# Threshold attention with a bilinear layer: two copies out of one product without an order between them, and loads of q and k that change places

## The chip, the cores and the metric

The kernel runs on one core of a Trainium2 chip. The metric is the device time of one execution in microseconds, as the median of several runs. A core has five engines that work side by side, each through its own instructions in order: PE (TensorE, matmuls; its loads of weights are listed as PEld), ACT (ScalarE), DVE (VectorE), POOL (GpSimd) and SP (SyncE, which issues nearly all transfers here). They wait for each other through semaphores.

## The reference

```python
def _attn_ref(q, k, v, tau):                 # 8 batches x 8 heads, 576 rows, 64 columns
    scale = 1.0 / np.sqrt(q.shape[-1])
    scores = scale * np.matmul(q, k.transpose(0, 1, 3, 2))
    thresh = np.max(scores, axis=-1, keepdims=True) - tau
    scores = np.where(scores >= thresh, scores, -1000000000.0)
    scores = scores - np.max(scores, axis=-1, keepdims=True)
    attn = np.exp(scores)
    attn = attn / (np.sum(attn, axis=-1, keepdims=True) + 1e-09)
    return np.matmul(attn, v)

def _moe_ref(x, w_a, w_b, w_out):            # x: 4608 x 512; w_a, w_b: 512 x 1536; w_out: 1536 x 512
    return (x @ w_a) * (x @ w_b) @ w_out
```

The attention's result, with the heads of a row side by side, is x. All numbers are fp32.

## The kernel before, in words

Two heads of a batch make a pair: 32 pairs, four to a batch. A pair's 576 rows of q are cut into units u = 0 to 3 of 128 rows and a last one of 64, the tail (u = 4). All matmuls are 64 x 64 tiles[...]. The main loop runs over slots g, one unit of attention each. In a set of four pairs there are 20 slots: first (pair, 0) and (pair, 1) for each of the four pairs in slots 0 to 7, then (pair, 2), (pair, 3), (pair, 4) for each in slots 8 to 19. The next set follows.

A slot's work in the order in which it is written:

- `scores` (L352): matmuls of qT and kT into two PSUM tiles sc (one for the tail); then on DVE the row maximum (L359) and the threshold (L360).
- `turn_blocks` for the unit of the slot before: DVE transposes its weights in 32 x 32 blocks (L446), SP writes them to DRAM (`swap`, L457). `turn_back` later reads them back as wT (L466, L469).
- a part of the bilinear layer (`advance`): matmuls into pab (L626, L699) and po (L756, L802), a share of them at four places of each slot, set by a pace.
- `weigh`: ACT's exp (L380), DVE's masking with the row sums (L383).
- `prep`: on DVE, the transposition (L320) in 32 x 32 blocks of rows of q or k that a later slot needs. Of a pair, q comes in two loads: q0 (rows for u = 0, 1; 128x256 in SBUF) and q1 (the rest; 128x320); k comes in one (128x576).
- `weighted`, where a part is due: the product of the turned weights with v into the PSUM tile pv (L483), 36 matmuls, and `settle`, which copies it into x. Parts are due three slots after units u = 1 and u = 4, that is in slots 4, 6, 8, 10 (a half of 256 rows) and 13, 16, 19 and 2 of the next set (the other half and the tail, 320 rows).
- the sums' reciprocals on DVE (L394, L396) and ACT's normalising (L402).
- `load` (L147): SP issues four transfers for q0, k or q1 of a later pair; `load_v` (L170); stores of results (L826).

Before the change, q0 of a pair is loaded four slots ahead of its first unit and turned two ahead; k is loaded three ahead and turned one ahead. The tiles of q rotate over two buffers, those of k over four.

All PSUM tiles (sc, pv, pab, po, tp) come from one pool of four tiles of two banks. A new tile waits for those who read the one whose place it takes. A part of the layer with seven products in place of eight holds up to two of the four over longer stretches.

`settle` takes pv in two halves: with its first half ACT fills the first columns of x's tile (L490), with the second half DVE fills the rest, in two copies of 64 rows, as the two heads stand crossed there (L492). Where a tail is due, `settle` is called twice on the same pv, for xT and for xt. The tile layer records an order between the copies of the two engines, since they touch the same tiles, so ACT goes first, then DVE, and with a tail ACT and DVE once more. When a batch's half of x is complete, POOL copies it with the two 64-row halves exchanged (xS, L500), for the layer.

At the end `keep_order` fixes the order on every engine as written.

Of the kernel before, what the change touches and what calls it, by code (L numbers as in the profile page):

```python
# [52 lines left out]
def kernel(  # L53
# [38 lines left out]
    nc = tc.nc  # L92
    B, H, S, D = q.shape
    P = 128
# [6 lines left out]
    TAIL = S - MAIN  # L101
# [7 lines left out]
    GT = HALF // TAIL  # L109
# [16 lines left out]
    def banks(n, name):  # L126

        return psum.tile([P, 2, 512], FP32, tag="banks", name=name)[:, :, 0:n]
# [152 lines left out]
    for _ in range(TW_BUFS):  # L281
        t = work.tile([P, 2 * NB, Q], FP32, tag="tw", bufs=TW_BUFS, name="rows")
# [31 lines left out]
    x_of, xtail_of = {}, {}  # L314
# [123 lines left out]
    def width(i, h):  # L438
        return (HALF, HALF, TAIL)[h] if i < HP else (HALF, HALF + TAIL)[h]
# [35 lines left out]
    def product(wT, vm, n):  # L475

        pv = banks(n // 2, "pv")
        for s in range(NSLOT):
            for j in range(2):
                rows = slice(j * D, (j + 1) * D)  # L480
                for c in range(2):
                    y = j ^ c
                    nc.tensor.matmul(pv[c * D:(c + 1) * D, y], vm[rows, s], wT[y](rows, s),  # L483
                                     start=(s == 0), stop=(s == NSLOT - 1))
        return pv

    def settle(out, pv, c0, c1):

        n = c1 - c0
        nc.scalar.copy(out[:, 0:n], pv[:, 0, c0:c1])  # L490
        for c in range(2):
            nc.vector.tensor_copy(out[c * D:(c + 1) * D, n:2 * n], pv[(1 - c) * D:(2 - c) * D, 1, c0:c1])  # L492

    def x_tile(name):
        return work.tile([P, HP, HALF], FP32, tag="xT", bufs=XT_BUFS, name=name)

    def exchange(x, xs, hp, c0, c1, engine):

        for r in range(2):
            engine.tensor_copy(xs[r * D:(r + 1) * D, hp, c0:c1], x[(1 - r) * D:(2 - r) * D, hp, c0:c1])  # L500
# [17 lines left out]
    def weighted_unit(i, u):  # L518

        b, hp = pairs[i]  # L520
        wT = turned.pop((i, u, "pe"))
        pv = product([lambda rows, s, t=t: t[rows, s] for t in wT], loaded[i]["v"], P)
        if (b, 0) not in x_of:
            x_of[b, 0] = x_tile("xT")
            state["xs"] = x_tile("xS")
        settle(x_of[b, 0][:, hp, u * P:(u + 1) * P], pv, 0, D)
        exchange(x_of[b, 0], state["xs"], hp, u * P, (u + 1) * P, nc.gpsimd)
        if hp == HP - 1:
            state["rows"] = u + 1
            if u == 0:  # L530
                blocks.append(((x_of[b, 0], state["xs"]), ("first", b, 0)))

    def weighted(i, h):

        b, hp = pairs[i]
        n = width(i, h)
        if h < 2:
            groups = G + (n > HALF)
            wT = [turned.pop((i, 2 * h + y))[:, 0:groups] for y in range(2)]
        else:  # L540
            t = turned.pop((i, NT))
            wT = [t[:, y:y + 1] for y in range(2)]
        pv = product([lambda rows, s, t=t: t[rows, :, s] for t in wT], loaded[i]["v"], n)
        if h < 2:
            if hp == 0:
                x_of[b, h] = x_tile("xT")
            settle(x_of[b, h][:, hp, :], pv, 0, P)
            if hp == HP - 1:
                complete.append((x_of.pop((b, h)), ("half", b, h)))
        if n % HALF:  # L550
            t = b % GT
            if hp == 0 and t == 0:
                xtail_of[b // GT] = x_tile("xt")
            settle(xtail_of[b // GT][:, hp, t * TAIL:(t + 1) * TAIL], pv, (n - TAIL) // 2, n // 2)
            del loaded[i], prepared[i]
            if hp == HP - 1 and t == GT - 1:
                complete.append((xtail_of.pop(b // GT), ("tail", b - t, 0)))
# [325 lines left out]
    def backlog():  # L883
        return (len(blocks) + len(complete)) * cost() + (running["left"] if running["ffn"] is not None else 0)
# [28 lines left out]
    n = 0  # L913
# [4 lines left out]
    for g in range(len(units) + PV_LAG):  # L918
        written = len(pending)
        state["converted"] = state["added"]  # L920
        here = g < len(units)
        converting = bool(early.get(g)) or bool(early.get(g - 1))
        if here:
            i, u = units[g]
            scores(i, u)
        exchange_blocks()
        pace = (PACE if g > BY_PE else PACE_EARLY) * BLOCK_COLS
        if g > BY_PE:
            pace = min(pace, backlog() / (min([a for a in arrivals if a > g] + [len(units) + PV_LAG + 1]) - g))
        pace += NSLOT * S / 2 / (NT + 1) + CATCH_UP * max(backlog() - BLOCK_COLS, 0)  # L930
        if 2 <= g < BY_PE + 2:
            weighted_unit(*units[g - 2])
            running["owed"] -= NSLOT * P // 2
        if g < 3:
            prep_copy(*prep_pe(g + 1, "q"))
        convert_rest(g, 0)
        if g == 0:
            for c in range(0, 2 * QUARTER - 2 * CW + 1, 2 * CW):
                extra.append(more_u32[:, c:c + 2 * CW].rearrange("p (f w) -> p f w", w=2))
        if g == 3:  # L940
            for c in range(0, NSUM - 2 * CW + 1, 2 * CW):
                extra.append(sums_u32[:, c:c + 2 * CW].rearrange("p (f w) -> p f w", w=2))
        load_weights(RAWS)
        if g > BY_PE and g <= len(units):
            turn_blocks(*units[g - 1])
        if g > BY_PE:
            advance(PORTIONS[0] * pace)
        if here:
            weigh(i, u)
        if here and g < BY_PE:  # L950
            reciprocal(i, u, nc.vector)
        if 0 < g <= BY_PE:
            turn_pe(*units[g - 1])
        if g < 3:
            prep_copy(*prep_pe(g + 1, "k"))
        for p in range(HP, NPR):
            for name, d in (("q0", 2), ("k", 1), ("q1", 1)):
                if g == (second if name == "q1" else first)[p] - d:
                    prep(p, name)
        if g > BY_PE:  # L960
            advance(PORTIONS[1] * pace)
            n = g - PV_LAG
            if BY_PE <= n < len(units) and part(*units[n]):
                p, h = part(*units[n])
                if pairs[p][1] == 0:
                    make_x(2 if h == 1 and p >= HP and pairs[p][0] % GT == 0 else 1)
                make_room()
                weighted(*part(*units[n]))
                running["owed"] -= NSLOT * width(*part(*units[n])) // 2
            if BY_PE + 1 < g <= len(units) + 1:  # L970
                turn_back(*units[g - 2])
        for n in early.get(g, [])[:1]:
            convert_first(n)
            convert_clamp(n)
        if here and g < BY_PE:
            diagonals(i, u)
        elif here:
            reciprocal(i, u, nc.scalar if converting else nc.vector)
            normalise(i, u)
        convert_rest(g, 1)  # L980
        if g <= BY_PE:
            advance(pace)
        convert_rest(g, 2)
        for n in early.get(g, [])[1:]:
            convert_first(n)
            convert_clamp(n)
        load_weights(RAWS)
        for p in range(HP, NPR):
            for name, d in (("q0", 4), ("k", 3), ("q1", 3)):
                if g == (second if name == "q1" else first)[p] - d:  # L990
                    load(p, name)
        for p in range(1, NPR):
            if g == first[p] - 1:
                load_v(p)
        if BY_PE <= g < BY_PE + HP:
            load_v(g - BY_PE, again=True)
        store(written)
        if g > BY_PE:
            advance(PORTIONS[2] * pace)
            advance(PORTIONS[3] * pace)  # L1000

        if not converting and not state["sums"]:
            state["slots"] = state.get("slots", 0) + 1
            for n in {1: (0,), 2: (1,), 3: (2,)}.get(state["slots"], ()):
                for z in range(2):
                    weight_sums(n, z)
            if state["slots"] >= 3 and state["through"]:
                for z in range(2):
                    weight_sums(3, z)
                state["sums"] = True  # L1010
        if g > first[HP] + 1 and not converting and state["first"] < 3 * SEVENS:
            first_sums(state["first"] % 3, state["first"] // 3)
            state["first"] += 1
# [37 lines left out]
```

## Time and profile before

| | |
|---|---|
| median of three runs | 1477.29 us (1473.63 to 1477.57) |
| the profiled execution | 1482.24 us, its span 1480.5 us |
| busy: PE, PEld | 1394.5 us (94%), 1257.0 us (85%) |
| busy: DVE, ACT, POOL | 1010.0 us (68%), 684.8 us (46%), 480.1 us (32%) |
| granted TensorE clock, mean | 0.988 |
| DMA | 223.21 MB, mean 151 GB/s |
| start (0 to 185 us): PE busy | 148.78 us |
| middle (185 to 1345 us): PE busy | 1116.03 us |
| end (1345 to 1480 us, the layer alone): PE busy | 129.66 us |

The span runs from the first to the last instruction; the execution's own time has the start and the end around it. A row of the costliest groups reads: line, engine, operation, tile written <- tiles read, shapes, count | busy time, mean length in ns | idle time of the engine ahead of these instructions, and what ended most of it. A row of waits reads: engine, line, what ended the wait, then the total, the count and the longest in us. A wait for several semaphores is put down to one of them. The lengths of matmuls are modelled, and they overlap.

### The profile page before, as it was taken

The page shows a single profiled execution, that of the slowest core. Times are in us where ns is not written, and L with a number is a line of the kernel's source. Part 1 is how long each engine was busy: PE and PEld are TensorE (multiplying, and loading weights), DVE is VectorE, ACT ScalarE, POOL GpSimd, SP SyncE. Part 2 cuts the span into 40 slices and gives each one's busy share as a digit, 9 for nine tenths or more (in the row PEclk, how much of TensorE's full clock was granted, in tenths as well). Part 3 has the DMA queues.
Part 4 walks back from the last instruction along what each step waited for, and adds up shares of the span by engine and source line. Part 5 has one row for each costly group of instructions (what it writes and reads, how often), then busy time and mean ns, then how long its engine had stood idle before and what let it go on. Part 6 is the DMA issues. An engine that isn't in the chain of part 4 may idle for free.

```text
span 1480.5 us, 76328 instructions
## 1 busy us (share of the span) xinstructions
PE 1394.5 (94%) x34208; PEld 1257.0 (85%) x34208; DVE 1010.0 (68%) x2245; ACT 684.8 (46%) x1243; POOL 480.1 (32%) x668
## 2 busy tenths in 40 slices
PE   5789999998999999999999899999999989999998
PEld 4678687887889988899998787988888968999998
DVE  5798687777867786586756577667766677654223
ACT  4787455545545454454444444445545445441110
POOL 2674623423060506033324224150505060605000
PEclk9899999999999999999999999999999999999999
DMA  9877677668756775577556676467755676551000
GB/s 211 201 206 189 164 172 191 170 163 194 176 147 157 169 199 149 138 171 180 144 131 139 151 171 165 117 171 163 188 140 141 166 176 169 136 137 41 4 18 17
DMA packets 325080, 223.21 MB, mean 151 GB/s; under 512 B 169616, under 2 KB 308880, under 8 KB 324752
## 3 DMA queue, kind: packets, MB, share of 16 engines
q1 hardware_dynamic: 322384, 217.73, 60.0%
q8 instruction: 269, 4.41, 1.3%
q10 hardware_dynamic: 2368, 0.59, 0.2%
q14 instruction: 59, 0.48, 0.1%
HBM read 128.58 MB, written 89.65 MB: 147 GB/s over the span
## 4 chain that ended last, share of the span: by engine, by line
PE 79%; DVE 6%; DMA 5%; issue 3%; SPq 3%; ACT 2%; POOL 1%; ACTq 0%; DVEq 0%; POOLq 0%
PE pab L626 25%; PE pab L699 18%; PE po L756 17%; PE pv L483 9%; PE sc L352 9%; DMA wT<-swap 2%; DVE mx L359 2%; SPq L457 1%; DMA kT<-in_k_dram 1%; DVE tw L446 1%; POOL kept L725 1%; PE po L802 1%; DVE xT L492 1%; PE tp L427 1%; DVE tw L383 0%
## 5 line engine op out<-in xcount | busy, mean ns | idle before, releaser
L402 ACT ACTIVATE tw<-tw,rcp 128x576 f32<-128x576 f32 x272 | 197.8, 769 | 219.0 <-DVE rcp L396 219.0
L359 DVE TENSOR_REDUCE mx<-sc 128x1 f32<-128x576 f32 x288 | 205.3, 749 | 125.2 <-PE sc L352 121.6
L380 ACT ACTIVATE tw<-sc,bias,scalars 128x576 f32<-128x576 f32 x288 | 239.4, 831 | 9.8 <-ACT bias L379 0.2
L592 POOL TENSOR_TENSOR h<-h,u 128x512 f32<-128x512 f32 x28 | 35.1, 1276 | 628.7 <-DVE h L669 491.0
L383 DVE SCALAR_TENSOR_TENSOR tw<-sc,thr,tw 128x576 f32<-128x576 f32 x288 | 223.6, 799 | 14.7 <-ACT tw L380 14.5
L756 PE MATMUL po<-wo_sb,h 64*64 64x256 f32 x3264 | 222.2, 377 | 0.0
L352 PE MATMUL sc<-kT,qT 64*64 64x288 f32 x2016 | 190.9, 405 | 17.2 <-ACT xt L490 6.8
L446 DVE STREAM_TRANSPOSE tw<-tw 128x576 f32<-128x576 f32 x272 | 196.1, 754 | 0.8 <-ACT tw L402 0.8
L483 PE MATMUL pv<-wT,vm 64*64 64x160 f32 (+3 forms) x5184 | 180.8, 274 | 12.1 <-DMA wT<-swap 7.7
L756 PEld LDWEIGHTS po<-wo_sb,h 64*64 64x64 f32 x3264 | 171.0, 133 | 20.9
L483 PEld LDWEIGHTS pv<-wT,vm 64*64 64x64 f32 x5184 | 164.6, 134 | 22.3 <-issue 9.9
L756 PE MATMUL po<-sums_u,h 64*64 64x256 f32 x2448 | 164.8, 379 | 2.5 <-DVE h L707 2.5
L725 POOL TENSOR_TENSOR h<-h 128x256 f32<-128x256 f32 x168 | 117.4, 731 | 115.8 <-PE po L756 101.9
L352 PEld LDWEIGHTS sc<-kT,qT 64*64 64x64 f32 x2016 | 112.2, 133 | 42.0 <-ACT xt L490 16.5
L756 PEld LDWEIGHTS po<-sums_u,h 64*64 64x64 f32 x2448 | 126.1, 134 | 19.5 <-DVE h L707 3.2
L492 DVE COPY xT<-pv 64x128 f32<-64x128 f32 (+1 forms) x136 | 38.1, 280 | 141.5 <-ACT xT L490 140.4
L626 PE MATMUL pab<-xU,wb_sb 64*64 64x128 f32 x4096 | 133.3, 270 | 0.3 <-issue 0.2
L626 PEld LDWEIGHTS pab<-xU,wb_sb 64*64 64x64 f32 x4096 | 126.6, 133 | 3.7 <-issue 0.7
L379 ACT ACTIVATE bias<-mx,scalars 128x1 f32<-128x1 f32 x288 | 82.9, 288 | 91.2 <-DVE mx L359 90.9
L626 PE MATMUL pab<-xS,wa_sb 64*64 64x128 f32 x2048 | 110.7, 270 | 3.1 <-POOL xS L500 1.5
L490 ACT COPY xT<-pv 128x128 f32<-128x128 f32 (+1 forms) x68 | 17.6, 260 | 202.8 <-PE pv L483 202.7
L699 PE MATMUL pab<-xS,wb_sb 64*64 64x256 f32 (+1 forms) x1536 | 100.1, 363 | 0.0
(137 smaller groups left out, 2427.2 us busy)
## 6 DMA issues: line engine op xcount, KB each, us to landing
swap<-tw SPq DMA_DIRECT2D x480, 144.0 KB, 2.6
wT<-swap SPq DMA_DIRECT2D x120, 576.0 KB, 4.6
vm<-in_v_dram SPq DMA_DIRECT2D x128, 72.0 KB, 3.3
swap<-tw SPq DMA_DIRECT2D x128, 72.0 KB, 1.8
kT<-in_k_dram SPq DMA_DIRECT2D x112, 72.0 KB, 4.4
wT<-swap SPq DMA_DIRECT2D x56, 144.0 KB, 2.9
out_dram<-kept SPq DMA_DIRECT2D x30, 256.0 KB, 4.1
qT<-in_q_dram SPq DMA_DIRECT2D x112, 40.0 KB, 4.3
```

Source lines behind the costliest of these rows:

```text
L352: nc.tensor.matmul(sc[j if u < NT else 0][to, c], qT[r, q0:q0 + D], kT[r, c * SH:(c + 1) * SH], start=True, stop=True)
L359: nc.vector.tensor_reduce(mx[:, c], sc[j], axis=AX.XY, op=ALU.max)
L379: nc.scalar.activation(bias[:, j:j + 1], mx[:, j:j + 1], AF.Copy, scale=e_nscale)
L380: nc.scalar.activation(wb[j], sb[j], AF.Exp, bias=bias[:, j:j + 1], scale=e_scale)
L383: nc.vector.scalar_tensor_tensor(out=wv, in0=sb[j], scalar=thr[:, j:j + 1], in1=wv, op0=ALU.is_ge, op1=ALU.mult, accum_out=sums[:, j:j + 1])
L402: nc.scalar.activation(w, w, AF.Copy, scale=rcp[:, j:j + 1])
L446: nc.vector.transpose(w, w)
L483: nc.tensor.matmul(pv[c * D:(c + 1) * D, y], vm[rows, s], wT[y](rows, s), start=(s == 0), stop=(s == NSLOT - 1))
L626: nc.tensor.matmul(out[c * D:(c + 1) * D, r, f * P:(f + 1) * P], w[g][k][rows, w0:w0 + D], moving[k][rows], start=(fresh and k == 0 and f ...
L699: nc.tensor.matmul(pab[c * D:(c + 1) * D, r], w[rows, f // n, k, fs + c * D:fs + (c + 1) * D], moving, start=(k == 0), stop=(k == H - 1))
L725: (nc.vector if state["over"] else nc.gpsimd).tensor_tensor(*a, **kw)
L756: nc.tensor.matmul(po[c * D:(c + 1) * D, r, y], ht[rows, t0:t0 + D], other[rows, f], start=(f == 0), stop=(f == NF // 2 - 1))
```

## The change

The copies of `settle` are declared independent of each other where they are on different engines: ACT's copies and DVE's copies of one pv no longer wait for one another, also across the two calls for a half and a tail (they share the lists in `read`). Waits of the copies for the product, and of readers for the copies, stay. Then the slots: q0 is loaded three slots ahead of a pair's first unit and turned one ahead, k is loaded four ahead and turned two ahead. q1 stays.

```diff
-    def settle(out, pv, c0, c1):
+    def settle(out, pv, c0, c1, others):
 
         n = c1 - c0
-        nc.scalar.copy(out[:, 0:n], pv[:, 0, c0:c1])
-        for c in range(2):
-            nc.vector.tensor_copy(out[c * D:(c + 1) * D, n:2 * n], pv[(1 - c) * D:(2 - c) * D, 1, c0:c1])
+        one = [nc.scalar.copy(out[:, 0:n], pv[:, 0, c0:c1])]
+        two = [nc.vector.tensor_copy(out[c * D:(c + 1) * D, n:2 * n], pv[(1 - c) * D:(2 - c) * D, 1, c0:c1])
+               for c in range(2)]
+        for mine, theirs in ((one, others[1] + two), (two, others[0] + one)):
+            for a in mine:
+                for b in theirs:
+                    tc.declare_no_dep(a.ins, b.ins, reason="banks of their own")
+        others[0].extend(one)
+        others[1].extend(two)
...
-        settle(x_of[b, 0][:, hp, u * P:(u + 1) * P], pv, 0, D)
+        settle(x_of[b, 0][:, hp, u * P:(u + 1) * P], pv, 0, D, ([], []))
...
+        read = [], []
...
-            settle(x_of[b, h][:, hp, :], pv, 0, P)
+            settle(x_of[b, h][:, hp, :], pv, 0, P, read)
...
-            settle(xtail_of[b // GT][:, hp, t * TAIL:(t + 1) * TAIL], pv, (n - TAIL) // 2, n // 2)
+            settle(xtail_of[b // GT][:, hp, t * TAIL:(t + 1) * TAIL], pv, (n - TAIL) // 2, n // 2, read)
...
-            for name, d in (("q0", 2), ("k", 1), ("q1", 1)):
+            for name, d in (("q0", 1), ("k", 2), ("q1", 1)):
                 if g == (second if name == "q1" else first)[p] - d:
                     prep(p, name)
...
-            for name, d in (("q0", 4), ("k", 3), ("q1", 3)):
+            for name, d in (("q0", 3), ("k", 4), ("q1", 3)):
                 if g == (second if name == "q1" else first)[p] - d:
                     load(p, name)
```

## The prediction

> **What bounds the kernel now.** I read the page's busy shares first, then the windows of three stretches, the list of waits, and last the timeline at each wait of PE.
>
> ```profile
> PE 1394.5 (94%) x34208; PEld 1257.0 (85%) x34208; DVE 1010.0 (68%) x2245; ACT 684.8 (46%) x1243; POOL 480.1 (32%) x668
> ...
> L492 DVE COPY xT<-pv 64x128 f32<-64x128 f32 (+1 forms) x136 | 38.1, 280 | 141.5 <-ACT xT L490 140.4
> ...
> L490 ACT COPY xT<-pv 128x128 f32<-128x128 f32 (+1 forms) x68 | 17.6, 260 | 202.8 <-PE pv L483 202.7
> ```
>
> ```profile
> 185.00:1345.00 1160.00, 1116.03 (x27777) 1003.47 (x27773) 821.49 (x1840) 552.15 (x985) 363.70 (x531) 1.00 0.65 160
> ```
>
> PE is the bound, at a granted clock of 1.00 in the long middle stretch, where attention and layers run side by side. All that this change can win there are PE's pauses: 1160.0 - 1116.0 = 44 us. ACT waits for the product with v, and DVE then waits for ACT (140.4 us of idle). Most of that idle is the product itself; what matters is the end of the pair of copies, and who waits for it:
>
> ```profile
> PEld sc L352 <- ACT xt L490: 16.5, 8, 2.1
> ...
> PE sc L352 <- ACT xt L490: 6.8, 4, 1.7
> ...
> PE sc L352 <- DVE xt L492: 4.6, 3, 1.7
> ```
>
> The scores wait for the copies: their second PSUM tile takes the one that pv has just used. One such place in the timeline (start, length, engine, operation, idle before it):
>
> ```profile
> 307.20 0.27 ACT L490 COPY xT<-pv 128x128 f32<-128x128 f32 x1 [4.96 <-PE pv L483]
> 307.50 0.59 DVE L492 COPY xT<-pv 64x128 f32<-64x128 f32 x2 [2.55 <-ACT xT L490]
> ...
> 308.12 0.18 ACT L490 COPY xt<-pv 128x32 f32<-128x32 f32 x1 [0.66 <-DVE xT L492]
> 308.34 0.39 DVE L492 COPY xt<-pv 64x32 f32<-64x32 f32 x2 [0.25 <-ACT xt L490]
> ...
> 308.94 0.95 PE L352 MATMUL sc<-kT,qT 64*64 64x288 f32 x11 [1.61 <-ACT xt L490]
> ```
>
> The two engines work in strict turn, ACT, DVE, ACT, DVE, from 307.20 to 308.73, and PE goes on 0.2 us later. The wait is put down to ACT, but it is DVE's copy that ended last. The second pause that the change touches:
>
> ```profile
> 340.62 0.77 DVE L320 STREAM_TRANSPOSE kT<-kT 128x576 f32<-128x576 f32 x1
> ...
> 341.46 0.60 PEld L352 LDWEIGHTS sc<-kT,qT 64*64 64x64 f32 x12 [0.95 <-issue]
> ```
>
> The scores of a pair start when its keys are turned (340.62 + 0.77 = 341.39); the profile says "issue", but the end of the turn lies 0.07 us ahead.
>
> **What the Trainium skill says.** "PSUM — Partial Sum Buffer", section "Specifications (TRN2)": ScalarE and VectorE read PSUM in parallel at full bandwidth as long as they don't meet in one bank. ACT reads the first bank of pv, DVE the second. The trace before agrees for other tiles: ACT's exp out of sc at 339.01 (0.83 us, mean of its row 0.831) overlaps DVE's masking out of the other sc at 338.91 (0.80, mean 0.799). "Perfetto Trace Analysis", section "Optimization Strategy": the same gap coming back on the busiest engine can mean too few buffers for the next tile. The trace agrees: eight waits of some 2 us on ACT's xt copy, all at a tile that takes pv's PSUM. The same page, section "DMA Instruction — HWDGE (DVE, Sync)": a transfer's semaphore wait is spent on the issuing sequencer, ahead of the start that is shown, so what is queued behind it stands too. SP's wait at L147, shown below, agrees.
>
> **The change, part by part.**
>
> *A. The order between the copies goes.* No instruction is added or removed: 68 + 32 copies on ACT, 136 + 64 on DVE. DVE now waits for the product itself. In the place above DVE would run from 307.20: 0.59 + 0.02 + 0.39 = 1.00, to 308.20, while ACT needs 0.27 + 0.18 = 0.45. The last end falls from 308.73 to 308.20: **0.53 us** where a tail goes with the half (0.30 from the start, 0.23 from the turn in the middle); without a tail **0.30 us** (ACT's 0.27 and 0.03 of handing over). This needs a DVE that is idle when the product ends: its idle of 140.4 us in 61 waits is 2.3 us each, so it is, outside the first 100 us, where DVE is busy and 8 products gain next to nothing. I followed every pause of PE over 0.3 us in the timeline. It ends 0.10 to 0.22 us after the last copy in 14 places:
> - nine with a tail, at 308.94, 441.52, 599.77, 823.34, 853.13, 996.74, 1021.75, 1161.43 and 1302.57, each with 1.2 to 2.1 us between two matmul starts, so more than 0.53: 9 x 0.53 = 4.8 us;
> - five without, at 370.35, 528.15, 709.27, 922.00 and 1085.12 (0.34 to 1.34 us): 5 x 0.30 = 1.5 us.
>
> Indirect, where the copies are a link further back: POOL's exchange L500 waits for DVE's copy in 7 places (14.6 us) and PE then for xS, at most 7 x 0.30 = 2.1; from 210 to 262 us the chain that ended last passes through three settles (220.19, 234.93, 249.87) and on through DVE to the swap transfers, 3 x 0.30 = 0.9; four pauses that end on DVE's masking after such a slot (292.56, 314.17, 334.17, 630.24), 4 x 0.30 = 1.2. Together 0 to 4.2; I take half, 2.1, since POOL's copies and DVE's other work bound some of them.
>
> *B. Rows of q and keys change places.* On DVE a turn of q0 takes 0.44 (128x256) and one of k 0.77, 28 of each. Counting slots in a set of four pairs (20 slots), q0 was turned in slots 18, 0, 2, 4 and k in 19, 1, 3, 5; now the reverse. The turn that stands just ahead of a pair's first scores becomes 0.33 us shorter. That pause shows four times (341.49, 501.02, 661.03, 836.36, with 0.55 to 0.90 us): 4 x 0.33 = 1.3 us. The longer turn goes to the even slots. Queued behind it on DVE are the copies out of pv (slots 2 and 4), the sums and reciprocals and, through them, ACT's normalising. In slots 2 and 4 DVE stood idle for 0.8 us or more ahead of the product's end every time (least at 1037.6 and 1203.1), so 0.33 is covered; without that cover it would be 12 x 0.33 = 4 us at worst.
>
> On SP four issues of k (0.63 us each) and four of q0 (0.46) change places. Before, three of four q0 loads stood at SP for their buffer, which the next slot's scores still read:
>
> ```profile
> SPq L147 <- PE sc L352: 8.8, 9, 2.5
> ```
>
> A slot later that buffer is free, so these waits go. Queued behind them are the stores of results, and then the next slot's swaps, which wait for DVE anyway (L457 on L446, 331.9 us in 107 waits): I take 0, with bounds of 1 us gained and 1 us lost (the k issues take 4 x 0.17 = 0.7 us longer in three slots of 20 and as much less in the next, where v is loaded too). k has four buffers, freed at least three slots ahead. Landing: k, in the place that q0 takes, landed 3.5 us or more ahead of its turn each time (the closest landed at 322.29, turned at 325.81), and q0 is the smaller load; no wait on a landing comes in.
>
> *Sum.* 4.8 + 1.5 + 1.3 = 7.6 direct, 2.1 indirect. Of a pause removed, a part comes back: PE reaches the next wait sooner, and some of these (PE on wT<-swap, 13.3 us with the weights' side in 12 waits) hang on SP and transfers. I take back 2.2, three tenths of the direct sum. That leaves **-7.5 us**. The profiled execution has a span of 1480.5, 1482.24 with what lies around it, 5 us above the median of the three runs, 1477.29. The difference is put to the median: **1469.8**.
>
> **Rivals.**
> 1. *The gain comes back elsewhere (or the order isn't lifted, since both engines write one xT tile).* If the pauses move to the next wait, a third is left, -2.5; if only B acts, -1.3. Time 1474.8 to 1476.0. For it: DMA's mean busy share is 0.65 in the stretch, and PE still waits for transfers. Against it: those transfers start from DVE's turns, which follow the scores on PE, so the chain moves as a whole.
> 2. *Slower: two readers of pv hold each other up.* One mechanism: ACT and DVE read the two halves of pv and write one xT at the same time, which no trace of before shows for this tile. If DVE's two copies take twice as long (1.18 and 0.78), a settle with a tail ends after 1.98 instead of 1.53 us, one without after 1.18 instead of 0.89: 9 x 0.45 + 5 x 0.29 = 5.5, half as much again indirectly, less the 1.3 of B: +7 us, 1484. It decides from copies that are longer by half (0.30 of 0.59). Against it: the banks differ, and exp and masking overlap unhurt. Short of that point it takes from the gain only.
> 3. *More than forecast.* If all indirect links count and nothing comes back: -11.8, and 1 us from SP: 1464.5.
>
> **How the numbers follow.** A change under 0.3% (4.4 us) can't be told from none in this kernel, whose runs before differ by 3.9 us. The forecast case has 0.55, the third 0.12, the first 0.23, the second 0.10. Their own ends spread over the bound: faster 0.64, same 0.26, slower 0.10. For 8 in 10 the range takes in the third case with its spread of runs and most of the first: 1461 to 1478.
>
> **What would show it.** Right: DVE's row L491 (the copies' new line) waits for PE pv and no longer for ACT; the idle 18.4 us of ACT's xt for DVE's xT is gone; PE's pauses after a product with a tail fall from about 2.0 to 1.5 us; SP's wait at the loads for PE sc is near nothing; the four pauses behind the keys' turn are under 0.6 us. Wrong: copies longer than 0.28 us on DVE, or PE's idle of 44 us in the middle stretch unchanged, with larger rows for wT<-swap or DVE's masking.

## The result and the profile after

The changed kernel took **1464.73 us** (median of 6 runs, 1457.75 to 1467.37), the kernel before on the same chip 1476.54 us (6 runs, 1473.16 to 1477.57). The ratio is **0.992** [0.9896, 0.9945], 11.8 us less. Two further comparisons of the same two kernels, told below, gave 0.9939 [0.9918, 0.996] and 0.9942 [0.9919, 0.9966], 8.4 and 8.6 us less. The forecast was 1469.8, 7.5 us less.

The profiled execution of the changed kernel took 1467.37 us, its span 1465.6. First the busy shares, then two of the costliest groups (the copies of `settle` are now at L490 and L491):

```profile
PE 1387.9 (95%) x34208; PEld 1248.2 (85%) x34208; DVE 1014.9 (69%) x2245; ACT 682.9 (47%) x1243; POOL 479.5 (33%) x668
...
L491 DVE COPY xT<-pv 64x128 f32<-64x128 f32 (+1 forms) x136 | 38.1, 280 | 120.3 <-PE pv L483 119.1
...
L490 ACT COPY xT<-pv 128x128 f32<-128x128 f32 (+1 forms) x68 | 17.6, 258 | 206.0 <-PE pv L483 205.9
```

The counts are the same. DVE's copies have the same length (280 ns before and after), but what ends the idle time before them is now the product (119.1 us of it), not ACT: the order is gone, and the two readers of pv don't slow each other. This fits the Trainium skill, "PSUM — Partial Sum Buffer", section "Specifications (TRN2)", which has ScalarE and VectorE read PSUM in parallel at full bandwidth without a bank collision, now also for this tile.

The middle stretch by windows (length, then busy time of PE, PEld, DVE, ACT, POOL):

```profile
185.00:1335.00 1150.00, 1114.66 (x27736) 1012.14 (x27732) 823.99 (x1840) 549.50 (x984) 362.26 (x535) 1.00 0.65 161
```

PE is idle here for 1150.0 - 1114.7 = 35.3 us, where it was 44.0: 8.7 us less, at the same mean clock of 1.00. (The window ends 10 us sooner, as the stretch does.) In the two later profiles of the changed kernel it was 38.2 and 39.8 us, that is 5.8 and 4.2 less: the size differs from one execution to the next. From the ninth slot (slot 8) to the end, the span is 9.9 us shorter; the other 5.0 of the 14.9 us between the two spans lie ahead of slot 8, which began at 82.5 before and at 77.5 after. The granted clock (the third number from the end) was another in the first part of the run, as the windows from 40 to 80 us show, of before and of after:

```profile
40.00:80.00 40.00, 28.57 (x678) 25.14 (x678) 30.78 (x73) 28.50 (x60) 25.29 (x31) 0.87 0.85 194
```

```profile
40.00:80.00 40.00, 31.43 (x846) 27.07 (x848) 34.34 (x82) 32.64 (x70) 27.93 (x33) 0.96 0.93 226
```

0.96 in place of 0.87 over 40 us is 3.6 us at most, an estimate that takes PE to set the pace throughout; from 80 to 185 us it was 1.00 in place of 0.97. An experiment below asks whether the change has a part in it.

The waits of PE and PEld on the copies, and SP's at the loads:

```profile
PEld sc L352 <- ACT xt L490: 12.3, 8, 1.6
...
PE sc L352 <- ACT xt L490: 4.7, 4, 1.2
...
PE sc L352 <- DVE xt L491: 3.2, 3, 1.1
```

```profile
SPq L170 <- DMA wT<-swap: 13.2, 18, 1.2
...
SPq L147 <- PE sc L352: 2.3, 4, 1.2
```

The three rows have the same counts as before, and each wait is about half a microsecond shorter (longest 2.1 to 1.6, 1.7 to 1.2, 1.7 to 1.1). SP's wait at the loads for the scores fell from 8.8 us in 9 to 2.3 in 4, as forecast, but a wait later in the queue grew (L170, loads of v, 3.5 us in 4 before, 13.2 in 18 now), so that SP's waits at the two together did not fall.

The place of the timeline that the prediction showed, five microseconds sooner:

```profile
302.23 0.27 ACT L490 COPY xT<-pv 128x128 f32<-128x128 f32 x1 [4.97 <-PE pv L483]
302.23 0.59 DVE L491 COPY xT<-pv 64x128 f32<-64x128 f32 x2 [2.27 <-PE pv L483]
302.39 0.19 ACT L490 COPY xt<-pv 128x32 f32<-128x32 f32 x1
302.84 0.39 DVE L491 COPY xt<-pv 64x32 f32<-64x32 f32 x2
...
303.50 0.95 PE L352 MATMUL sc<-kT,qT 64*64 64x288 f32 x11 [1.13 <-ACT xt L490]
```

Both engines start at 302.23. DVE ends at 302.84 + 0.39 = 303.23, 1.00 us after the start in place of 1.53, and PE's idle is 1.13 in place of 1.61. The wait is still put down to ACT, which ended at 302.58; the copy that PE waits for is DVE's.

And the turn ahead of a pair's first scores, which is now one of q0:

```profile
334.49 0.44 DVE L320 STREAM_TRANSPOSE qT<-qT 128x256 f32<-128x256 f32 x1
...
335.00 0.67 PEld L352 LDWEIGHTS sc<-kT,qT 64*64 64x64 f32 x13 [0.61 <-issue]
```

The turn takes 0.44 in place of 0.77, and the idle time of PEld behind it is 0.61 in place of 0.95.

Of PE's pauses, taken as the time between two matmul starts, the same places add up so:

| pauses | before | after | less | forecast |
|---|---|---|---|---|
| 9 after a product with a tail | 17.5 us | 12.9 us | 4.6 us | 4.8 us |
| 5 after one without | 3.74 us | 2.50 us | 1.24 us | 1.5 us |
| 4 behind the turn of a pair | 2.75 us | 1.37 us | 1.4 us | 1.3 us |

### The profile page after: what moved, and what is told of

Its sections match the earlier page's. It is cut to its first block, busy times and chain, and to the rows that moved or that the text cites. A ratio compares the mean times of both kernels' runs of the same rounds, so it can differ in the third digit from the quotient of the medians.

```text
span 1465.6 us, 76332 instructions
## 1 busy us (share of the span) xinstructions
PE 1387.9 (95%) x34208; PEld 1248.2 (85%) x34208; DVE 1014.9 (69%) x2245; ACT 682.9 (47%) x1243; POOL 479.5 (33%) x668
## 4 chain that ended last, share of the span: by engine, by line
PE 78%; DVE 7%; DMA 5%; SPq 5%; issue 3%; ACT 1%; POOL 1%; ACTq 0%; DVEq 0%; POOLq 0%
PE pab L633 24%; PE pab L706 18%; PE po L763 17%; PE pv L483 9%; PE sc L352 9%; DMA wT<-swap 2%; SPq L457 2%; DVE mx L359 2%; SPq L147 1%; DMA qT<-in_q_dram 1%; DVE tw L446 1%; DVE tw L383 1%; PE po L809 1%; SPq L225 1%; POOL kept L732 0%
## 5 line engine op out<-in xcount | busy, mean ns | idle before, releaser
L352 PE MATMUL sc<-kT,qT 64*64 64x288 f32 x2016 | 192.0, 405 | 10.5 <-ACT xt L490 4.7
L446 DVE STREAM_TRANSPOSE tw<-tw 128x576 f32<-128x576 f32 x272 | 196.0, 754 | 0.8 <-ACT tw L402 0.8
L763 PEld LDWEIGHTS po<-wo_sb,h 64*64 64x64 f32 x3264 | 167.4, 133 | 24.9
L491 DVE COPY xT<-pv 64x128 f32<-64x128 f32 (+1 forms) x136 | 38.1, 280 | 120.3 <-PE pv L483 119.1
L490 ACT COPY xT<-pv 128x128 f32<-128x128 f32 (+1 forms) x68 | 17.6, 258 | 206.0 <-PE pv L483 205.9
```

What stands on the lines that cost most here:

```text
L352: nc.tensor.matmul(sc[j if u < NT else 0][to, c], qT[r, q0:q0 + D], kT[r, c * SH:(c + 1) * SH], start=True, stop=True)
L446: nc.vector.transpose(w, w)
L763: nc.tensor.matmul(po[c * D:(c + 1) * D, r, y], ht[rows, t0:t0 + D], other[rows, f], start=(f == 0), stop=(f == NF // 2 - 1))
```

## The experiments

All ratios are against the kernel before, run on the same chip in the same rounds. The changed kernel ran twice more among them (`e3_changed_again`, `e12_changed_control`), so that the experiments of the first and the last group can be held against it. The four runs from `e5_halves_apart` to `e8_layer_between` had no changed kernel beside them; they are held against `e12_changed_control`, which ran on the same chip later.

**Each part alone.** `e1_copies_only` keeps the free copies and puts the slots of the loads and turns back:

```diff
-            for name, d in (("q0", 1), ("k", 2), ("q1", 1)):
+            for name, d in (("q0", 2), ("k", 1), ("q1", 1)):
...
-            for name, d in (("q0", 3), ("k", 4), ("q1", 3)):
+            for name, d in (("q0", 4), ("k", 3), ("q1", 3)):
```

> The copies are independent, q0 and keys stay in their old places. Theory (the change is the sum of two separate gains, most of it from copies that end 0.53 or 0.30 us sooner): faster than before by 8 to 11 us, PE's pauses after a product with a tail 1.5 us as in the changed kernel, but the four pauses behind the keys' turn stay at 0.55 to 0.9 us. Rival (the moved loads and turns carry the gain, through SP's queue): within 4 us of before.

`e2_moves_only` does the reverse: `settle` as before, the slots as changed.

```diff
-            for name, d in (("q0", 2), ("k", 1), ("q1", 1)):
+            for name, d in (("q0", 1), ("k", 2), ("q1", 1)):
...
-            for name, d in (("q0", 4), ("k", 3), ("q1", 3)):
+            for name, d in (("q0", 3), ("k", 4), ("q1", 3)):
```

> Only q0 and keys change places, the copies stay ordered. Theory: 1 to 2 us faster than before, which can hardly be told from none; the four pauses behind the turn shorter by 0.33 us, those after a product with a tail still about 2.0 us. Rival (SP's queue): 5 us faster or more.

And the whole change on the chip of these two:

> The changed kernel once more, on the same chip as the two halves, so that their sum can be compared with it. Theory: -11 to -13 us against before, equal to the sum of the two halves within 3 us. Rival (the two parts need each other, or pay each other back): it differs from the sum by more than 4 us.

Measured: copies alone 1472.8 us, 0.9963 [0.9945, 0.9981], 5.5 us less; moves alone 1481.02, 1.0009 [0.999, 1.0027], no gain; both 1469.33, 0.9939 [0.9918, 0.996], by the ratio 9.0 us less. All three fell short of what was expected (8 to 11, 1 to 2, 11 to 13 us). In the traces each part does its own work: with the copies alone 13 of the 14 pauses at products are as after the change and the four behind turns as before (0.90, 0.64, 0.65, 0.53); with the moves alone the pauses with a tail are as before, and of the four behind turns two became shorter (0.56, 0.22) and two longer (0.98, 1.00). So lifting the order of the copies gains by itself, and the moves by themselves don't. By the ratios the parts alone add up to 4.2 us less, the whole to 9.0. That the moves are worth something together with the free copies is suggested by this and not settled, with intervals of some 2 to 3 us to each side.

**The start.** The changed kernel came to slot 8 five microseconds sooner. `e4_start_ordered` keeps the order between the copies in the 8 products of the start only:

```diff
+        if others is None:
+            return
         for mine, theirs in ((one, others[1] + two), (two, others[0] + one)):
...
-        settle(x_of[b, 0][:, hp, u * P:(u + 1) * P], pv, 0, D, ([], []))
+        settle(x_of[b, 0][:, hp, u * P:(u + 1) * P], pv, 0, D, None)
```

> As the changed kernel, but the eight products of the start (64 columns each) keep ACT's copy ahead of DVE's. The trace after stands 4.9 us ahead of the one before already in slot 8, at about 82 us. Theory A (that lead is chance of one execution: at most three of these copies could start sooner): within 2 us of the changed kernel, and the lead at slot 8 varies among kernels without regard to the order there. Theory B (the copies of the start carry it): 4 to 5 us slower than the changed kernel, and slot 8 begins as late as before.

Measured: 1468.59 us, 0.9938 [0.9913, 0.9962], and slot 8 at 78.5 us: the lead is there without the free copies at the start. It goes with the clock granted in the execution that was profiled. From 20 to 40 and from 40 to 80 us it was 0.87 and 0.87 in the kernel before (slot 8 at 82.5), 1.00 and 0.83 with the moves alone (81.8), 1.00 and 0.87 with the copies alone (79.5), 1.00 and 0.91 here (78.5) and in the changed kernel's second profile (79.1), 0.88 and 0.96 in its first (77.5). One more profile has the change at clocks like those of before: `e8_layer_between`, whose own edit acts only later, had 0.87 and 0.87 and came to slot 8 at 81.6 us, 0.9 ahead of the kernel before. So these 5.0 us of the two profiles are mostly not the change's; how much of the first comparison's 11.8 us is of this kind can't be told from one profile, but the two later ones gave 3 us less.

**The turn in the middle.** The prediction split 0.53 us into 0.30 at the start and 0.23 for the second exchange between the half and the tail. `e5_halves_apart` frees the copies within each call of `settle`, but keeps the order between the two calls:

```diff
-        read = [], []
...
-            settle(x_of[b, h][:, hp, :], pv, 0, P, read)
+            settle(x_of[b, h][:, hp, :], pv, 0, P, ([], []))
...
-            settle(xtail_of[b // GT][:, hp, t * TAIL:(t + 1) * TAIL], pv, (n - TAIL) // 2, n // 2, read)
+            settle(xtail_of[b // GT][:, hp, t * TAIL:(t + 1) * TAIL], pv, (n - TAIL) // 2, n // 2, ([], []))
```

> Each call of the copies is independent within itself, but a tail's copies still wait for the other engine's copies of the half before it. Theory (0.23 of the 0.53 us come from the turn in the middle): pauses of PE after a product with a tail about 1.75 us, between before (2.0) and the changed kernel (1.5), and 2 to 3 us slower than the changed kernel. Rival (all that counts is that DVE starts sooner): pauses of 1.5 us and the same time.

Measured: 1470.43 us, 0.9934 [0.991, 0.9957], as the whole change; eight of the nine pauses with a tail are 1.42 to 1.60 us, not 1.75 (1.40 to 1.59 in the changed kernel). The timeline of this kernel at the place shown above:

```profile
303.40 0.27 ACT L490 COPY xT<-pv 128x128 f32<-128x128 f32 x1 [5.21 <-PE pv L483]
303.40 0.59 DVE L491 COPY xT<-pv 64x128 f32<-64x128 f32 x2 [2.51 <-PE pv L483]
304.02 0.39 DVE L491 COPY xt<-pv 64x32 f32<-64x32 f32 x2
304.02 0.18 ACT L490 COPY xt<-pv 128x32 f32<-128x32 f32 x1 [0.36 <-DVE xT L491]
...
304.62 0.95 PE L352 MATMUL sc<-kT,qT 64*64 64x288 f32 x11 [1.09 <-ACT xt L490]
```

ACT does wait for DVE (0.36), but DVE goes straight on at 304.02, because ACT's xT, the only one it must wait for, ended at 303.67. The order between the calls binds ACT alone, which has time. Here only the order that makes DVE wait costs anything; lifting it within each call is enough.

**SP's queue, first part.** The prediction put the moved loads at nothing. `e6_q0_loaded_early` is the changed kernel with q0 loaded where it was before, in the same slot as k and ahead of it:

```diff
-            for name, d in (("q0", 3), ("k", 4), ("q1", 3)):
+            for name, d in (("q0", 4), ("k", 4), ("q1", 3)):
```

> As the changed kernel, but q0 is loaded four slots ahead, where it stands at SP for its buffer; turns as in the changed kernel. Theory (SP's wait at these loads is covered): SP's wait at the loads for the scores comes back to some 8 us and the time stays within 1.5 us of the changed kernel. Rival (SP's queue carries a part of the gain): 3 us slower or more.

Measured: 1479.23 us (14 runs, 1469.98 to 1487.64), 1.0009 [0.9987, 1.0032]. **The expectation failed**: the whole gain was gone, though the four short turns and all free copies were in place. This is neither the order of before nor that of the changed kernel: the eight loads of q0 and k stand in one slot, one behind the other. SP waited 14.2 us in 17 at the loads for the scores.

**A cost doubled.** `e7_copies_twice` lets DVE make each of its copies twice, one after the other, with the same values:

```diff
-               for c in range(2)]
+               for _ in range(2) for c in range(2)]
```

> As the changed kernel, with each of DVE's copies out of the product made twice (the same values again). Theory (14 pauses of PE end on the last copy, and what is indirect follows): a pause with a tail is longer by 0.98 us, one without by 0.59, so 9 x 0.98 + 5 x 0.59 = 11.8 us slower than the changed kernel at least, up to 18 with indirect links and further pauses that come above zero. Rival (the gain came from elsewhere and the copies are covered): under 4 us slower.

Measured: 1497.82 us, 1.0115 [1.0085, 1.0146], some 26 us more than the change (1.0115 - 0.994 of 1479), above the expectation. Eight of the nine pauses with a tail went up by 1.05 to 1.15 us each (0.98 were expected), to 2.5 to 2.7. But PE's pauses after copies became more in number as well, by about ten of over 0.2 us, and rose from about 18 to about 35 us together. The list of waits shows the new ones under "issue", which hides them:

```profile
PEld sc L352 <- issue: 39.5, 34, 3.0
```

That row of the changed kernel holds 5.9 us in 16. A microsecond more on DVE at each product costs more than the places that already paused; one less gains only at these. So the gain of the change could not have been read from the cost of its opposite. These pauses are some 17 of the 26 us. Another part goes with the granted clock, 0.989 in the mean of these runs and 0.993 in those of `e12_changed_control`: an estimate of 6 us at most (0.004 of 1498).

**Other work into the pause.** The layer's share that a slot owes is set before the scores come. `e8_layer_between` lets the part of the layer ahead of the waiting scores run at full share and deducts the product's work at the end of the slot:

```diff
-        written = len(pending)
+        written, later = len(pending), 0
...
-                running["owed"] -= NSLOT * width(*part(*units[n])) // 2
+                later = NSLOT * width(*part(*units[n])) // 2
...
             advance(PORTIONS[3] * pace)
+            running["owed"] -= later
```

> As the changed kernel, but the columns of a product with v are taken off the layer's account at the end of the slot and not right after the product, so that layer matmuls stand between a product and the next slot's scores. Theory (the copies' remaining 1.5 us pause after a product is only bare because the scores follow it at once): most of the nine pauses of 1.5 us go, 8 to 15 us faster than the changed kernel. Rival (layer matmuls moved there are missing elsewhere, and products wait for swapped weights or the scores come late for DVE): within 4 us of the changed kernel, or slower.

Measured: 1495.27 us, 1.0105 [1.0077, 1.0134]. The pauses after copies nearly vanish, from about 18 to under 4 us, but the kernel is some 25 us slower than the changed one where 8 to 15 us faster were expected, and the rival was right. PE now waits elsewhere: pauses behind turns on DVE went from under 3 to some 14 us, those for POOL's exchange from some 6 to some 12:

```profile
PEld pab L633 <- POOL xS L506: 10.2, 12, 3.1
...
PEld sc L352 <- issue: 25.4, 36, 2.2
```

The same rows of the changed kernel hold 5.1 us in 12 and 5.9 in 16. The layer's work that fills a pause is missing where it hid another. PE's idle from 185 to 1335 us is 47.0 us here and was 35.3 to 39.8 in three profiles of the changed kernel, so these waits account for a part of the 25 us; where the rest arises is not traced.

**SP's queue, second part.** Where did the gain of `e6_q0_loaded_early` go? Three kernels ran together. `e9_turns_not_moved` issues the loads in the order of the changed kernel and leaves the turns where they were before the change:

```diff
-            for name, d in (("q0", 1), ("k", 2), ("q1", 1)):
+            for name, d in (("q0", 2), ("k", 1), ("q1", 1)):
...
                 turn_back(*units[g - 2])
+        for p in range(HP, NPR):
+            if g == first[p] - 3:
+                load(p, "q0")
...
-            for name, d in (("q0", 3), ("k", 4), ("q1", 3)):
+            for name, d in (("k", 4), ("q1", 3)):
```

> The copies are independent and the loads stand in SP's order exactly as in the changed kernel (q0 issued three slots ahead, after the slot's read of the swapped weights; keys four ahead), but DVE turns q0 two slots ahead and the keys one ahead, as before. Copies alone gave -0.37%, the whole change -0.6 to -0.8%. Theory (the missing part is SP's: q0 no longer stands in SP's queue for its buffer): within 0.15% of the changed kernel less the 1.3 us of the shorter last turn, so about -0.5% or better against before. Rival (the missing part is DVE's, through the order of the turns): -0.37%, as the copies alone.

`e10_q0_loaded_early_2` is the kernel of `e6_q0_loaded_early` again:

> The kernel with q0 loaded four slots ahead once more, for a second profile: its first profile fell on its fastest run. Its runs lay 0.7% above the changed kernel, where 1.5 us had been expected. Theory (SP stands at q0 for the scores with eight loads in a row, and the next slot's swaps come late): in a run near the median the wait of SP at the loads is again 10 us or more, and PE's pauses at products with v for swapped weights are longer by 5 us or more than in the changed kernel. Rival (a spread of runs by chance): a median within 0.3% of the changed kernel.

And the changed kernel as their control:

> The changed kernel on the same chip as the three others, to compare with. -0.6 to -0.8% against before.

Measured: loads moved and turns not, 1471.55 us (22 runs), 0.9948 [0.9931, 0.9966]; q0 early, 1481.31 us (20 runs, 1473.61 to 1493.52), 1.0028 [1.0009, 1.0047]; the changed kernel 1470.44, 0.9942 [0.9919, 0.9966]. The turns' part is thus too small to be seen in the time. The interval of the kernel with the loads moved also takes in the -0.37% of the copies alone, so that this comparison does not settle what the moved loads are worth. The place of q0's loads moves the time by 0.9% (13 us) with everything else the same. SP's wait at the loads with q0 early, then PE's for weights that come back from DRAM, in the second profile:

```profile
SPq L147 <- PE sc L352: 16.2, 15, 2.1
```

```profile
PE pv L483 <- DMA wT<-swap: 15.0, 10, 3.1
```

and the second row in the control:

```profile
PE pv L483 <- DMA wT<-swap: 8.6, 8, 2.9
```

(PEld's rows, 15.5 and 8.3, cover in part the same stretches of time and are not added.) The expectation asked for a profile near the median; this one fell on the longest of the 20 runs. In the first profile of the same kernel, of the shortest of its 14 runs, PE's row has 10.2 us, and in the two other profiles of the changed kernel 8.0 and 11.3, so a longer wait for weights is seen in the second profile alone. One place of the second profile in the timeline, q0 early first, then the changed kernel at the same place (times from each span's start):

```profile
337.86 1.43 DVE L446 STREAM_TRANSPOSE tw<-tw 128x576 f32<-128x576 f32 x2
...
338.13 1.98 SPq L147 DMA_DIRECT2D qT<-in_q_dram  x4
...
340.16 3.80 SPq L147 DMA_DIRECT2D kT<-in_k_dram  x4
...
344.06 2.07 SPq L457 DMA_DIRECT2D swap<-tw  x4
...
349.47 0.76 PE L483 MATMUL pv<-wT,vm 64*64 64x160 f32 x2 [2.32 <-DVE kept L473]
...
350.64 2.68 PE L483 MATMUL pv<-wT,vm 64*64 64x160 f32 x36 [0.41 <-DMA wT<-swap]
```

```profile
331.06 1.43 DVE L446 STREAM_TRANSPOSE tw<-tw 128x576 f32<-128x576 f32 x2
...
331.26 3.16 SPq L147 DMA_DIRECT2D kT<-in_k_dram  x4
...
334.52 2.70 SPq L457 DMA_DIRECT2D swap<-tw  x4
...
340.27 2.84 PE L483 MATMUL pv<-wT,vm 64*64 64x160 f32 x69
```

The weights were turned at 337.86 + 1.43 = 339.29 and at 332.49. SP issued their first write at 344.06, 4.8 us later, behind eight loads; in the changed kernel at 334.52, 2.0 us later, behind four. PE's wait of 2.32 us at the product is put down to DVE's add out of po, which ended at 349.36; the first weights landed at 349.38, so both were late, and the second half of the weights held PE once more at 350.64. SP's issues follow one another here without a pause, and the four of k take 3.80 us in place of 3.16 in themselves; these lines don't say why. Elsewhere a wait of a load holds the queue too, q0 early first, then the control at the same place:

```profile
1023.09 0.38 SPq L466 DMA_DIRECT2D wT<-swap  x1
1025.54 2.70 SPq L147 DMA_DIRECT2D qT<-in_q_dram  x4
1028.30 3.65 SPq L147 DMA_DIRECT2D kT<-in_k_dram  x4
1032.36 1.77 SPq L457 DMA_DIRECT2D swap<-tw  x4
```

```profile
1014.31 2.96 SPq L147 DMA_DIRECT2D kT<-in_k_dram  x4
1019.35 1.77 SPq L457 DMA_DIRECT2D swap<-tw  x4
```

SP issues nothing for some 2 us ahead of 1025.54, until the scores have read q0's buffer; this is one of the waits of the row above. The weights of that slot were turned at 1028.53, and their first write was issued at 1032.36, 3.8 us later; in the control they were turned at 1019.32 and the write was issued at 1019.35. This agrees with the Trainium skill, "Perfetto Trace Analysis", section "DMA Instruction — HWDGE (DVE, Sync)": the wait is spent on the sequencer, ahead of the start that is shown.

From each trace, the time from the end of the weights' turn (L446) to the first swap issue (L457), over the 140 or 141 units whose turn ends after the first 185 us (the 11 or 12 ahead of that add 37 to 44 us in every kernel):

| kernel | together | over 1.5 us late |
|---|---|---|
| before | 74 us | 19 |
| copies alone | 77 us | 20 |
| moves alone | 51 us | 13 |
| loads moved, turns not | 55 us | 15 |
| changed (three profiles) | 65 to 66 us | 14 to 18 |
| q0 early (two profiles) | 86 and 90 us | 27 and 28 |
| copies twice | 41 us | 11 |

The late ones lie in slots 17 to 19 and 0 to 6 of a set, where loads and turns for the next pairs are. Lateness alone doesn't give the time: the moves alone have less of it than the changed kernel and gain nothing, and of the two profiles of q0 early, the first (86 us late, PE idle for 37.0 us from 185 to 1335 us) has a span of 1468.2, the second (90 us, 49.2) one of 1491.7. The runs of that kernel also spread more widely: their standard deviation is 5.1 and 5.4 us in the two sets, and 2.8 to 3.9 in each of the four kernels that ran beside the second. Its longer runs have a lower mean granted clock (0.988 at 1493.52 us, 0.996 at 1473.61), but over all runs the mean clock of the two kernels is the same (0.9928 and 0.9934), so the clock doesn't account for the 0.9% between them.

It does have a part in the spread. In all the traces the granted clock is either 1 or 0.5, and it is 0.5 for 3.4 or 6.8 us at a time. Two windows of the second profile of q0 early, the first up to the product shown above, the second from there on (PE, PEld, DVE, ACT, POOL, then the clock):

```profile
345.90:349.30 3.40, 1.25 (x23) 0.70 (x15) 3.40 (x8) 1.71 (x4) 2.17 (x3) 1.00 0.90 235
349.30:356.10 6.80, 6.22 (x81) 5.21 (x85) 0.35 (x2) 0.31 (x2) 4.50 (x10) 0.50 0.53 125
```

PE paused, and then it ran for 6.8 us at half the clock. The 14 profiles have 64 such stretches, leaving aside the one at the end of each span. Ahead of every one PE had been busy for at most 0.56 of the 3.4 us before; of all stretches of 3.4 us from 185 to 1335 us only 1 to 3 in 100 are as empty. This suggests that a pause of PE can cost it time once more, behind the pause. After the first 185 us the second profile of q0 early has 17.1 us at half the clock and the first 3.4, which is worth 7 us at most of the 23.5 between their spans, an estimate that takes PE to set the pace there. Shown is that the order of the loads costs 0.7 to 0.9% and that the swaps then go later. That the late swaps are what costs the time is argued; what decides in a single execution how many of them reach PE stays open.

**Half of the tail to ACT.** ACT ends long before DVE. `e11_tail_shared` gives it one of the two crossed copies of the tail, 64x32, which still waits for the copy that DVE makes of the same rows for the half:

```diff
...
+            if second and c == 1:
+                one.append((nc.scalar.copy(to, rows), c))
+            else:
+                two.append((nc.vector.tensor_copy(to, rows), c))
...
```

> As the changed kernel, but of a tail's two crossed copies ACT makes one[...]. DVE's work at a product with a tail falls from 0.98 to 0.79 us, ACT's rises from 0.45 to 0.64. Theory (the last copy sets the pause): pauses with a tail 1.3 us in place of 1.5, and 2 to 5 us faster than the changed kernel. Rival (ACT's wait for DVE, or its queue, takes the place): pauses of 1.5 us and the time of the changed kernel.

Measured: 1469.81 us (10 runs), 0.994 [0.9919, 0.9961], against 0.9942 of the control. Eight of the nine pauses with a tail fell as expected, from between 1.40 and 1.59 to between 1.12 and 1.31 us; in the timeline (the two tail copies, then the scores):

```profile
301.32 0.18 ACT L496 COPY xt<-pv 64x32 f32<-64x32 f32 x1
301.47 0.18 DVE L498 COPY xt<-pv 64x32 f32<-64x32 f32 x1
...
301.87 0.95 PE L352 MATMUL sc<-kT,qT 64*64 64x288 f32 x11 [0.91 <-ACT xt L496]
```

Some 0.28 us at eight of the nine places (the ninth was shorter already) is 2.2 us, below what these runs can tell. The expected 2 to 5 us do not show, and the two kernels are level.

## Why the prediction was right, point by point

- **A, direct: right in kind and size.** 6.3 us were forecast at the 14 pauses and 5.8 found (4.6 + 1.24), at the places that were listed. `e1_copies_only` ties it to the free copies, with a time 5.5 us lower (2.8 to 8.1 by its interval), where 8 to 11 were expected.
- **A, the split of the 0.53: wrong.** "0.30 from the start, 0.23 from the turn in the middle" gave the second exchange a price of its own. `e5_halves_apart` keeps that order and loses nothing: once DVE starts together with ACT, what it must wait for in the middle is long done.
- **B on DVE: right.** 1.4 us at the four turns for 1.3. No pause showed the longer turns in the even slots when both parts were in place; with the moves alone two of the four turn pauses got longer (0.98 and 1.00), and so did the same two with the copies made twice (0.99 and 1.00), a case that the prediction did not have.
- **B on SP: the ground was wrong, the size is not settled.** "I take 0, with bounds of 1 us gained and 1 us lost", since the swaps wait for DVE anyway (331.9 us in 107 waits). That sum over all slots hid the stretch that matters: mostly in slots 17 to 6 the swaps go out behind their turn already, by 74 us in all. With q0's loads beside k's, the change gained nothing (1.0009 and 1.0028 against 0.9942), a difference of 10 to 13 us, so the order of these loads is no free choice. What the move is worth against the kernel before is smaller: copies alone 5.5 us, with the loads moved 7.7 (0.9948 of 1479), on two chips and with overlapping intervals, so some 2 us or none. The prediction also took SP's waits to go; those for the scores did, but SP's waits at the loads of v rose from 3.5 to 13.2 us.
- **Indirect and taken back (2.1 and 2.2): not measured one by one.** Their sum, next to nothing, is within what was found: the three rows of the table above are 7.2 us, and PE's idle in the middle fell by 8.7, 5.8 and 4.2 us in the three profiles of the changed kernel. POOL's wait for DVE's copy fell from 14.6 us in 7 to 10.5 in 5, but PE's pauses for xS stayed (5.5 and 5.8): that link gave nothing. The waits for weights stayed too: PE's row on wT<-swap has 8.0 us after and 7.7 before. (The prediction's 13.3 us add PEld's row to it, though the two overlap in time; as stretches of time they cover 9.7.)
- **Rival 1, the gain comes back elsewhere: refuted.** PE's idle in the middle fell, by 8.7, 5.8 and 4.2 us in the three profiles, and the kernel was faster by more than the 1.3 to 2.5 us of this rival in all three comparisons.
- **Rival 2, two readers of pv slow each other: refuted** by the copies' 280 ns. `e7_copies_twice` shows that its price was too low: DVE's copies at twice their time cost 26 us against the changed kernel, where the rival had some 14 (from 1469.8 to 1484), in part because further pauses come above zero.
- **Rival 3, more than forecast (-11.8):** the first comparison gave exactly this figure, but not for its reasons. The two others gave 8.4 and 8.6, nearer the forecast, and the first profile's lead of 5 us ahead of slot 8 goes with the granted clock. That the first comparison met this figure is luck.

## What to carry to other kernels

When two engines empty one tile, ask which of them is last and free that one: the order that bound the faster engine cost nothing here. A row that says that a queue mostly waits for its data is no cover for the slots in which it doesn't; look at the queue slot by slot before a transfer is moved on it, above all ahead of a round trip that the busiest engine waits for. And price a stall in the direction of the edit: taking a microsecond away gains at the pauses that are there, while adding one makes new ones.

## What was not expected of the hardware

- A store of turned weights that sits behind eight loads in SP's queue was issued 4.8 us after its data were ready, behind four loads 2.0 us. The issues of k took 0.8 and 0.95 us each there, where the prediction reckoned with 0.63; why is not shown.
- The mean granted clock from 40 to 80 us differs from one profile to the next, also of one kernel (0.91 to 0.96 in three of the changed kernel, 0.83 to 0.96 over all 14), and slot 8 comes sooner or later with it: 77.5 to 79.1 us in those three, 82.5 in the one profile of the kernel before.
- The clock was never anything but 1 or 0.5, and each of the 64 stretches at 0.5 came behind 3.4 us in which PE had been busy for at most 0.56 of the time.
- The runs of q0 early spread more widely (standard deviations of 5.1 and 5.4 us) than those of the kernel before (3.9) and the changed kernel (2.8) on the same chip. What sets this off is known only in part.
